# Reordered weight copies and splits around the first two experts of an attention, routing and expert kernel, with later float-form jobs and a shorter mask set-up

## The chip, the cores and the metric

The kernel runs on one core of a Trainium2 chip. The metric is the device time of one execution in microseconds (us). Engines are named as in the profile: PE (TensorE, matmuls), PEld (its weight loads), DVE (VectorE), ACT (ScalarE), POOL (GpSimd) and SP (SyncE, which here only issues DMAs). Each engine works through its own list of instructions in the order in which the program was written.

## What is computed

Cut to what matters, the reference is a gated linear attention, a routed layer of eight experts, and a dense layer:

```python
# attention: B=2, H=8, S=768, D=48
for t in range(S):
    state = alpha[:, :, t, :, None] * state + einsum('bhd,bhe->bhde', k[:, :, t], v[:, :, t])
    y[:, :, t] = einsum('bhd,bhde->bhe', q[:, :, t], state)
x = y as 1536 tokens of 384 numbers
# routing: E=8 experts, each with F=1024 hidden units
e(i) = argmax(x[i] @ w_gate);  g(i) = its softmax weight
out[i] = g(i) * (relu(x[i] @ w1[e]) @ w2[e])      # tokens over an expert's capacity give 0
# dense layer, 384 -> 2048 -> 384
h = out @ w_in
result = (h * tanh(softplus(h))) @ w_out
```

## The kernel before, in words

Everything is float32. A product of two float32 numbers is made on PE from three products of shorter ones: each operand is split into a high part and a low part, and high times high, low times high and high times low are added up. A weight **piece** of 128x768 numbers is loaded into a tile `st[i]`; ACT copies it to its high part `whi[i]` (`conv_high`, L337 to L345), DVE subtracts the two and leaves the low part `wlo[i]` (`conv_low`, L347 to L350). Each expert has eight pieces, the even ones for its first product (`w1`), the odd ones for its second (`w2`); each serves two steps.

The program has three parts.

- **Attention and routing.** Twelve tiles of 128 tokens go through the attention and get an expert and a place. ACT writes a check value for each tile into `chk`. The rows of x, scaled by the gate, are scattered to a table `tab` in DRAM, sorted by expert. The last tile's share of expert 0 doesn't go through DRAM: PE adds it with matmuls of a one-hot matrix (`slot_split`, L846), on a split of the last tile's rows that ACT (`xg_lh`, L838) and DVE (`xg_ll`, L839) make.
- **Experts.** For each expert e a window of 240 rows is gathered from `tab` (`gather`, issued on SP, L124), transposed on PE (L1072) and split into `xh` (ACT, L1089) and `xl` (DVE, L1090), all of it by `xpose(e)`. Then come eight **steps** (e, m). A step issues `g1(e, m)` (nine matmuls at L1100, into one PSUM bank of two that alternate), whose result ACT turns into `hh` (L1104) and DVE into `hl` (L1105), and `g2` of three steps earlier (nine matmuls at L1117, which need that step's `hh` and `hl`). Steps are counted 0 to 63.
- **Dense layer.** `f1` (L1181) and `f2` (L1224) on pieces 64 to 79. `f_mish` (L1193 to L1199 on ACT) and `gated(b)` (L1209 to L1211 on DVE) stand between them; the first steps of `f1` overlap the last expert's.

Work that isn't tied to a step is slipped in by hand. The program turns off the scheduler (`manual_schedule`), so the order in which the Python code calls things is the order on each engine:

- The weights of the dense layer come as 64-bit words and are brought to **float forms** by twelve jobs. `cvt_a(n)` is ACT's Square (L198) and Relu (L233) and two bit operations on DVE (L201, L204); `cvt_b(n)` is one more bit operation on DVE (L209) and a store to DRAM (L241, tensors `wi_s` and `wo_s`) issued on SP. The list `free` (L1353) gives the steps that may take a job, and the jobs are spread over them.
- `load_to` (L327) issues the loads `st[i]` on SP (L331). Pieces 64 to 71 are read from `wi_s` and `wo_s`, so `load_to` holds back pieces 68 to 71 until all twelve `cvt_b` are issued (`written`, L324).
- `check_tiles` (L782) reduces `chk` on DVE to one number per partition, `cm`; `check_all` (L789), called in step 7, transposes `cm` on PE (L791) and reduces it further, for a flag that is read near the end.
- `tot` (L1055) is a small matmul that counts tokens per expert; `mxc`, `places` and `sort_places` turn it into offsets on DVE.

Of the kernel before, what the change touches and what calls it, by code (L numbers as in the profile page):

```python
# [10 lines left out]
F32 = mybir.dt.float32  # L11
# [4 lines left out]
AF = mybir.ActivationFunctionType  # L16
ALU = mybir.AluOpType
AX = mybir.AxisListType
# [5 lines left out]
def kernel(  # L24
# [18 lines left out]
    nc = tc.nc  # L43
# [3 lines left out]
    E = w1.shape[0]  # L47
# [5 lines left out]
    NTILE = NT // C  # L53
    HP = H // 2
    HS = 64
    R2 = HS + D
    SW = 2 * D + E
    KD = DM // 128
    MF = FF // 128
# [6 lines left out]
    ATT = 4  # L66
# [8 lines left out]
    const = ctx.enter_context(tc.tile_pool(name="const", bufs=1))  # L75
# [8 lines left out]
    def w_new(i):  # L84
        p = wr_p[2 if i >= 76 else (i + 8) % 12 < 8]
        whi[i], wlo[i] = (p.tile([128, PW], F32R, tag=t, name=f"{t}{i}") for t in ("whi", "wlo"))
# [135 lines left out]
    def cvt_load(n):  # L222
        if n < len(cvt_jobs):
            t = words(fpool[0].tile([128, 2 * CN], F32, tag="big", name="w64", bufs=3)[:, 0:2 * cvt_jobs[n][1].shape[1]])
            nc.sync.dma_start(out=t, in_=words(cvt_jobs[n][0]))
            cvt_t[n] = [t]
# [94 lines left out]
    ahead = [WST + 4]  # L321
# [5 lines left out]
    def load_to(n):  # L327
        while load_n[0] < min(n, len(pieces)) and cvt_n[0] >= written(load_n[0]):
            i = load_n[0]
            st = raw_p[i % 14 >= 8].tile([128, PW], F32, tag="st", name=f"st{i}")  # L330
            nc.sync.dma_start(out=st.rearrange("p (a b) -> p a b", b=pieces[i].shape[2]), in_=pieces[i])  # L331
            wst_t[i] = st
            load_n[0] += 1

    low = []

    def conv_high(n):  # L337
        while conv_n[0] < min(n, len(pieces)):
            i = conv_n[0]
            load_to(i + 1 + ahead[0])  # L340
            w = wst_t.pop(i)
            w_new(i)
            nc.scalar.activation(out=whi[i], in_=w, func=AF.Copy)  # L343
            low.append((i, w))
            conv_n[0] += 1  # L345

    def conv_low(only=None):  # L347
        for i, w in [x for x in low if only in (None, x[0])]:
            nc.vector.tensor_tensor(out=wlo[i], in0=w, in1=whi[i].bitcast(F32), op=ALU.subtract)  # L349
            low.remove((i, w))  # L350
# [13 lines left out]

    with ExitStack() as actx:
        ap_ = actx.enter_context(tc.tile_pool(name="att", bufs=1))
        chk = ap_.tile([128, NTILE], F32, name="chk")
        nc.vector.memset(chk, 0.0)
        neg1 = ap_.tile([128, 1], F32, name="neg1")
        nc.vector.memset(neg1, -1.0)  # L370
# [2 lines left out]
        sel = ap_.tile([128, HP, SW], F32, name="sel")  # L373

        tri_f = ap_.tile([128, 128], F32, name="tri_f")
        seen_f = ap_.tile([128, 128], F32, name="seen_f")
        seen = ap_.tile([128, 128], I32, name="seen")
        io_i = ap_.tile([128, E], I32, name="io_i")
        slot_i = ap_.tile([128, WIN], I32, name="slot_i")
# [1 line left out]
        def route_consts():  # L381
            nc.gpsimd.memset(tri_f, 1.0)
            nc.gpsimd.affine_select(
                out=tri_f, in_=tri_f, pattern=[[1, 128]], compare_op=ALU.is_gt,
                fill=0.0, base=0, channel_multiplier=-1,
            )
            nc.gpsimd.memset(ones, 1.0)
            nc.gpsimd.memset(seen_f, -1.0)
            nc.gpsimd.affine_select(
                out=seen_f, in_=seen_f, pattern=[[1, 128]], compare_op=ALU.is_ge,  # L390
                fill=0.0, base=0, channel_multiplier=-1,
            )
            nc.gpsimd.iota(io_i, pattern=[[-1, E]], base=E - 1, channel_multiplier=0)
            nc.gpsimd.iota(slot_i, pattern=[[1, WIN]], base=(E - 1) * NT, channel_multiplier=0)
            nc.gpsimd.iota(tokid, pattern=[[C, NTILE]], base=0, channel_multiplier=1)

        def route_copies():
            nc.scalar.activation(out=tri, in_=tri_f, func=AF.Copy)
            nc.scalar.activation(out=seen, in_=seen_f, func=AF.Copy)
            nc.scalar.activation(out=down, in_=io_i, func=AF.Copy)  # L400
            nc.scalar.activation(out=firsts, in_=io_i[0:1], func=AF.Copy, scale=float(NT))
            nc.scalar.activation(out=slots, in_=slot_i, func=AF.Copy)
# [64 lines left out]
        def heads(t):  # L467
            return t.rearrange("p (j c) -> p j c", j=HP)
# [45 lines left out]

        def k_scale(i):
            kp = sp.tile([128, HP, C], F32, tag="kp", name="kp")
            nc.vector.scalar_tensor_tensor(
                out=kp[0:R2], in0=heads(kn_t.pop(i))[0:R2], scalar=-1.0 if i == NTILE - 1 else 1.0,
                in1=rt_t.pop(i)[0:R2], op0=ALU.mult, op1=ALU.mult,
            )  # L520
            kp_t[i] = kp

        def q_scale(i):
# [258 lines left out]
        def check_tiles():  # L782
            ok = const.tile([128, NTILE], F32, name="ok")
            nc.vector.tensor_scalar(out=ok, in0=chk, scalar1=NEWTON_TOL, scalar2=None, op0=ALU.is_le)
            cm = const.tile([128, 1], F32, name="cm")
            nc.vector.tensor_reduce(out=cm, in_=ok, axis=AX.X, op=ALU.min)
            return cm
# [63 lines left out]
        def slot_hot(i):  # L851
            last = i == NTILE - 1
            hot_t[i] = mid_tile("hot_last")[:, 0:WIN].bitcast(F32R) if last else ap_.tile([128, WIN], F32, name=f"hot{i}")
            nc.vector.tensor_scalar(out=hot_t[i], in0=slots, scalar1=sl_l[i], scalar2=None, op0=ALU.is_equal)
# [186 lines left out]
        low_x = split_x(i)  # L1041
        route_rank(i)
        slot_hot(i)
        low_x()
        route_x(i)
        route_slot(i)
        cm = check_tiles()
        count(i + 1)
        route_c(SLOT1)
        conv_high(ATT - 1)  # L1050
        conv_low(0)
        slot_split()
        del xs_t[0]
        tot = rk[:, E:2 * E]
        nc.tensor.matmul(out=tot, lhsT=ones, rhs=pre[pre_n[0] % 2], start=True, stop=True, skip_group_check=True)  # L1055


    wr_p.append(main.enter_context(tc.tile_pool(name="wr1", bufs=8)))
# [77 lines left out]
    def y_out(e):  # L1136
        y_put(4 + e % 2 * 2, off_v.pop(e), free=e == E - 1)
# [8 lines left out]
    def places():  # L1146
        nc.vector.tensor_tensor_scan(out=inc, data0=tot, data1=zn[:, 0:E], initial=0.0, op0=ALU.add, op1=ALU.add)
        nc.vector.tensor_tensor(out=off, in0=inc, in1=tot, op=ALU.subtract)
        nc.vector.tensor_copy(out=meta_i, in_=off)
        nc.vector.scalar_tensor_tensor(out=inc, in0=down, scalar=-float(NT), in1=off, op0=ALU.mult, op1=ALU.add)  # L1150
# [191 lines left out]
    CVT_END = 45  # L1342
    LATE_AHEAD = 3
    xpose(0, False)
    nc.vector.tensor_reduce(out=mxc, in_=tot, axis=AX.X, op=ALU.max)
    conv_low(2)
    conv_high(ATT)
    scatter(tab, si_last, xg_last, E * NT, "tab")
    gather(1)
    pend = []  # L1350
    job_at = {}

    free = [s for s in range(3, E * MF) if s % MF != 5 and (s % MF != 2 or s < MF)]  # L1353
    for n in range(2 * len(cvt_jobs)):
        job_at.setdefault(free[n * CVT_END // (2 * len(cvt_jobs))], []).append(((cvt_a, cvt_b)[n % 2], n // 2))
    for e in range(E):
        for m in range(MF):
            step = e * MF + m
            if m == 6:
                off_v[e] = place(e)  # L1360
            g1(e, m)
            pend.append((e, m))
            if len(pend) > LAG:
                pe, pm = pend.pop(0)
                g2(pe, pm)
                if pm == MF - 1:
                    y_out(pe)
            if e == E - 1 and m >= MF - EARLY:
                n = m - MF + EARLY
                (f_head if m < MF - 1 else f1_at)(n)  # L1370
            conv_high(min(step + 1 + LEAD, ATT + step * 9 // 8, E * NP1 + 3))
            if step:
                conv_low({1: 1, 2: 4}.get(step))
            for f, n in job_at.get(step, ()):
                f(n)
                if f is cvt_b:
                    cvt_load(n + 3)
            if step == 4:
                places()
            if step == 5:  # L1380
                sort_places()
            if step == 7:
                check_all(cm)
                slow_at()
            if step % 4 == 3 and 0 < step // 4 <= NTILE:
                tok_scatter(step // 4 - 1)
            if e == E - 1 and m == 0:
                nc.sync.dma_start(
                    out=srt, in_=toks.rearrange("(c p) o -> p (c o)", p=128), allow_slow_non_contiguous=True
                )  # L1390
            if E * MF - EARLY - 1 - LATE_AHEAD <= step < E * MF - EARLY - 1:
                late_load(step - (E * MF - EARLY - 1 - LATE_AHEAD))
            if step == E * MF - 4:
                cvt_marks()
            if step == E * MF - 2:
                cvt_flag()
            if m == (5 if e else 6) and e + 1 < E:
                xpose(e + 1)
                if e + 2 < E:
                    gather(e + 2)  # L1400
    for pe, pm in pend:
# [242 lines left out]
```

## Time and profile before

| | us |
|---|---|
| median of 3 runs (lowest to highest) | 421.44 (421.35 to 422.85) |
| the profiled execution's own time | 421.35 |
| its span in the profile | 419.6 |
| PE busy | 406.4 (97%) |
| PE weight loads busy | 374.5 (89%) |
| DVE busy | 323.9 (77%) |
| ACT busy | 324.5 (77%) |
| POOL busy | 58.6 (14%) |
| chain that ended last | PE 89%, DVE 5%, ACT 2% |

The span is the time between the first and the last instruction that the profiler saw; 1.75 us of the execution lie around it. A busy share is an average over the three parts of the program. The attention part lasts to about 70 us, the experts from about 75 to 217 us, and the dense layer and the output from there to the end.

### The profile page before, as it was taken

What the parts mean: (1) busy time and instruction counts of PE and PEld (TensorE: products, weight loads), DVE (VectorE), ACT (ScalarE), POOL (GpSimd) and SP (SyncE); (2) the same over time, 40 slices, a digit from 0 to 9 for tenths busy, and PEclk for the clock granted to TensorE, in tenths of its full rate; (3) what the DMA queues carried; (4) which work ended last, traced back from release to release, by engine and by line L of the source; (5) the groups of instructions that cost most, each with busy time, mean ns of one, the idle gap of its engine ahead of it and who ended that gap; (6) DMA issues with size and microseconds to landing.
All of it is one profiled execution on the core that took longest, in us unless ns stands there. A gap on an engine that the chain in (4) does not pass through costs nothing.

```text
span 419.6 us, 8354 instructions
## 1 busy us (share of the span) xinstructions
PE 406.4 (97%) x3111; PEld 374.5 (89%) x3114; DVE 323.9 (77%) x645; ACT 324.5 (77%) x572; POOL 58.6 (14%) x77
## 2 busy tenths in 40 slices
PE   7899999899999999999999999999999999999993
PEld 3798998899999999999999899989898988889893
DVE  7999997899989888988649877867786775565361
ACT  5889997877868677777499987888788869797630
POOL 5222573101101012100000000000000000012043
PEclk9999999999999999999999999999999999999998
DMA  7999996999999999944525000211110000001022
GB/s 236 351 290 334 347 382 224 352 354 235 341 322 285 303 313 283 287 128 125 187 80 174 15 1 0 52 63 39 37 41 1 0 2 0 2 19 57 2 77 80
DMA packets 50541, 67.31 MB, mean 160 GB/s; under 512 B 5372, under 2 KB 41212, under 8 KB 50492
## 3 DMA queue, kind: packets, MB, share of 16 engines
q1 hardware_dynamic: 48572, 61.97, 47.9%
q0 software_dynamic: 1920, 4.73, 3.1%
q8 instruction: 26, 0.43, 0.4%
q14 instruction: 23, 0.19, 0.1%
HBM read 55.86 MB, written 10.83 MB: 159 GB/s over the span
## 4 chain that ended last, share of the span: by engine, by line
PE 89%; DVE 5%; ACT 2%; issue 1%; DMA 1%; POOL 0%; POOLq 0%; DVEq 0%; ACTq 0%
PE bk L1224 24%; PE bk L1181 24%; PE bk L1117 14%; PE bk L1100 14%; PE bk L537 3%; PE bk L589 2%; PE bk L605 2%; PE bk L578 2%; DVE wlo L349 1%; PE bk L557 1%; PE bk L613 1%; PE bk L1072 1%; DMA an<-in_alpha_t_dram 1%; DVE hl L1105 0%; PE bk L868 0%
## 5 line engine op out<-in xcount | busy, mean ns | idle before, releaser
L349 DVE TENSOR_TENSOR wlo<-st,whi 128x768 fp32r<-128x768 f32 x72 | 68.2, 953 | 12.4 <-ACT whi L343 9.9
L1209 DVE TENSOR_TENSOR p<-p,bk 128x512 f32<-128x512 f32 x48 | 32.8, 683 | 43.6 <-ACT p L1199 43.6
L1224 PE MATMUL bk<-whi,big 128*128 128x384 f32 x240 | 66.4, 337 | 0.0
L343 ACT ACTIVATE whi<-st 128x768 fp32r<-128x768 f32 x72 | 60.1, 841 | 0.0
L1193 ACT ACTIVATE p<-bk 128x512 f32<-128x512 f32 x48 | 28.8, 599 | 32.0 <-PE bk L1181 28.6
L1117 PE MATMUL bk<-hl,whi 128*128 128x240 f32 x192 | 52.9, 276 | 0.0
L1117 PE MATMUL bk<-hh,wlo 128*128 128x240 f32 x192 | 52.7, 275 | 0.0
L1117 PE MATMUL bk<-hh,whi 128*128 128x240 f32 x192 | 52.7, 274 | 0.0
L1224 PEld LDWEIGHTS bk<-whi,big 128*128 128x128 f32 x240 | 44.1, 188 | 1.5
L1104 ACT ACTIVATE hh<-bk 128x240 fp32r<-128x240 f32 x64 | 23.5, 367 | 28.2 <-PE bk L1100 25.3
L108 POOL DMA_INDIRECT out_dram<-acc,srt x12 | 12.2, 1018 | 225.5 <-DVE acc L1248 221.1
L1181 PE MATMUL bk<-x2l,whi 128*128 128x512 f32 x144 | 41.6, 397 | 0.0
L1181 PE MATMUL bk<-x2h,wlo 128*128 128x512 f32 x144 | 41.2, 394 | 0.0
L1181 PE MATMUL bk<-x2h,whi 128*128 128x512 f32 x144 | 41.1, 394 | 0.0
L1224 PE MATMUL bk<-wlo,big 128*128 128x384 f32 x120 | 40.6, 338 | 0.0
L1117 PEld LDWEIGHTS bk<-hl,whi 128*128 128x128 f32 x192 | 36.4, 189 | 0.2 <-DVE hl L1105 0.2
L1117 PEld LDWEIGHTS bk<-hh,whi 128*128 128x128 f32 x192 | 36.3, 189 | 0.0
L1117 PEld LDWEIGHTS bk<-hh,wlo 128*128 128x128 f32 x192 | 36.3, 189 | 0.0
L1100 PE MATMUL bk<-xh,whi 128*128 128x240 f32 x192 | 33.0, 280 | 1.7 <-ACT xh L1089 1.6
L1181 PEld LDWEIGHTS bk<-x2h,wlo 128*128 128x128 f32 x144 | 27.0, 188 | 6.7
L1181 PEld LDWEIGHTS bk<-x2l,whi 128*128 128x128 f32 x144 | 27.0, 188 | 6.4
L1100 PE MATMUL bk<-xl,whi 128*128 128x240 f32 x192 | 32.1, 276 | 0.4 <-DVE xl L1090 0.4
(238 smaller groups left out, 955.4 us busy)
## 6 DMA issues: line engine op xcount, KB each, us to landing
st<-in_w_dram SPq DMA_DIRECT2D x64, 384.0 KB, 7.9
qn<-in_q_t_dram SPq DMA_DIRECT2D x12, 256.0 KB, 5.4
kn<-in_k_t_dram SPq DMA_DIRECT2D x12, 256.0 KB, 7.1
w<-in_w_in_dram SPq DMA_DIRECT2D x6, 512.0 KB, 7.4
w<-in_w_out_dram SPq DMA_DIRECT2D x6, 512.0 KB, 6.4
sd<-in_w_in_dram SPq DMA_DIRECT2D x8, 384.0 KB, 4.1
sd<-in_w_out_dram SPq DMA_DIRECT2D x8, 384.0 KB, 4.7
tab<-zero SPq DMA_DIRECT2D x4, 720.0 KB, 6.5
```

Source lines behind the costliest of these rows:

```text
L108: r = nc.gpsimd.indirect_dma_start(out=dst[:, :], out_offset=bass.IndirectOffsetOnAxis(ap=idx, axis=0), in_=src, in_offset=None, bounds_ch ...
L343: nc.scalar.activation(out=whi[i], in_=w, func=AF.Copy)
L349: nc.vector.tensor_tensor(out=wlo[i], in0=w, in1=whi[i].bitcast(F32), op=ALU.subtract)
L537: nc.tensor.matmul(out=sc_t[i][r][:, j], lhsT=kp[p, j, :], rhs=qq[p, j, :], start=True, stop=True)
L578: nc.tensor.matmul(out=ot_at(j, r), lhsT=s2f[half(r), j * D:j * D + w], rhs=q2[i % 2][half(r), j, :], start=(j % 2 == 0), stop=False, skip ...
L1100: nc.tensor.matmul(out=hps, lhsT=a[:, kk], rhs=b_[:, kk, :], start=(n == 0), stop=(n == 3 * KD - 1))
L1104: nc.scalar.activation(out=hh, in_=hps, func=AF.Relu)
L1117: nc.tensor.matmul(out=y[n], lhsT=a[:, ns], rhs=b_, start=(m == 0 and t == 0 and n % 2 == 0), stop=(m == MF - 1 and t == 2), skip_group_ch ...
L1181: r = nc.tensor.matmul(out=hps, lhsT=a[:, kk], rhs=b_[:, kk, w0:w0 + wd], start=(n == 0), stop=(n == 3 * KD - 1))
L1193: nc.scalar.activation(out=p, in_=h2_t[b], func=AF.Sigmoid, scale=-1.0)
L1209: nc.vector.tensor_tensor(out=g, in0=g, in1=h2_t.pop(b), op=ALU.mult)
L1224: nc.tensor.matmul(out=o_t[c], lhsT=a[:, ts], rhs=b_, start=(m in (0, MA) and n == 0), stop=(m in (MA - 1, MF2 - 1) and n == 2),)
```

## The change

The changed kernel computes the same, with these edits:

- The body of `conv_high` becomes a function `high(i)`, so that pieces can be taken out of order. In the front (the stretch between the last tile of the attention and the first expert) ACT copies piece 2 between `xg_lh` and `xg_l`, piece 1 after `xpose(0)`, and piece 3 in step 0. On DVE `wlo[0]` is made before the count.
- The `tot` matmul goes from the front to behind `g1(0, 0)`, the reduction `mxc` to step 4.
- The jobs for float forms start at step 5 of the list `free`, not 3, and are spread over the same number of places: the first `cvt_a` is in step 6, the last `cvt_b` goes from step 60 to step 63.
- `xpose(1)` stands right behind `g2` in step 6, ahead of that step's weight copy; `place(0)` goes from step 6 to step 7.
- `check_tiles` is called in step 7, just ahead of `check_all`, not in the front.
- `k_scale` (L515) uses a plain multiply for all tiles but the last; the mask `seen` is built as int32 on POOL, without a float mask and ACT's copy.

```diff
+    def high(i):
+        load_to(i + 1 + ahead[0])
+        w = wst_t.pop(i)
+        w_new(i)
+        nc.scalar.activation(out=whi[i], in_=w, func=AF.Copy)
+        low.append((i, w))
+        conv_n[0] += 1
+
     def conv_high(n):
         while conv_n[0] < min(n, len(pieces)):
...
+            high(conv_n[0])
...
-        chk = ap_.tile([128, NTILE], F32, name="chk")
+        chk = const.tile([128, NTILE], F32, name="chk")
...
-            nc.gpsimd.memset(seen_f, -1.0)
+            nc.gpsimd.memset(seen, -1)
             nc.gpsimd.affine_select(
-                out=seen_f, in_=seen_f, pattern=[[1, 128]], compare_op=ALU.is_ge,
-                fill=0.0, base=0, channel_multiplier=-1,
+                out=seen, in_=seen, pattern=[[1, 128]], compare_op=ALU.is_ge,
+                fill=0, base=0, channel_multiplier=-1,
             )
...
-            nc.scalar.activation(out=seen, in_=seen_f, func=AF.Copy)
...
-            nc.vector.scalar_tensor_tensor(
-                out=kp[0:R2], in0=heads(kn_t.pop(i))[0:R2], scalar=-1.0 if i == NTILE - 1 else 1.0,
-                in1=rt_t.pop(i)[0:R2], op0=ALU.mult, op1=ALU.mult,
-            )
+            kn, rt = heads(kn_t.pop(i))[0:R2], rt_t.pop(i)[0:R2]
+            if i < NTILE - 1:
+                nc.vector.tensor_tensor(out=kp[0:R2], in0=kn, in1=rt, op=ALU.mult)
+            else:
+                nc.vector.scalar_tensor_tensor(out=kp[0:R2], in0=kn, scalar=-1.0, in1=rt, op0=ALU.mult, op1=ALU.mult)
...
         slot_hot(i)
+        high(2)
         low_x()
         route_x(i)
         route_slot(i)
-        cm = check_tiles()
+        conv_low(0)
         count(i + 1)
         route_c(SLOT1)
-        conv_high(ATT - 1)
-        conv_low(0)
         slot_split()
         del xs_t[0]
         tot = rk[:, E:2 * E]
-        nc.tensor.matmul(out=tot, lhsT=ones, rhs=pre[pre_n[0] % 2], start=True, stop=True, skip_group_check=True)
...
     xpose(0, False)
-    nc.vector.tensor_reduce(out=mxc, in_=tot, axis=AX.X, op=ALU.max)
     conv_low(2)
-    conv_high(ATT)
+    high(1)
     scatter(tab, si_last, xg_last, E * NT, "tab")
     gather(1)
...
-    free = [s for s in range(3, E * MF) if s % MF != 5 and (s % MF != 2 or s < MF)]
+    free = [s for s in range(5, E * MF) if s % MF != 5 and (s % MF != 2 or s < MF)]
...
-            if m == 6:
+            if m == (6 if e else 7):
                 off_v[e] = place(e)
...
+            if step == 6:
+                xpose(1)
...
+            if step == 0:
+                nc.tensor.matmul(out=tot, lhsT=ones, rhs=pre[pre_n[0] % 2], start=True, stop=True, skip_group_check=True)
             if step == 4:
+                nc.vector.tensor_reduce(out=mxc, in_=tot, axis=AX.X, op=ALU.max)
                 places()
...
             if step == 7:
-                check_all(cm)
+                check_all(check_tiles())
                 slow_at()
...
             if m == (5 if e else 6) and e + 1 < E:
-                xpose(e + 1)
+                if e:
+                    xpose(e + 1)
                 if e + 2 < E:
                     gather(e + 2)
```

What the edits do to the order on the engines shows at three places. Line numbers of the changed program are a few lower or higher than before; the operations are the same.

**The front, ACT.** The rows run from `xg_lh` to the first `hh` of the experts. Before:

```order
L838 ACTIVATE xg_lh_180<-bk3_89,gt_1307 128x384
L764 ACTIVATE xg_l1_169<-bk3_89,gt_1307 128x384
L343 ACTIVATE whi1_1326<-st1_791 128x768
L343 ACTIVATE whi2_1329<-st2_793 128x768
L1089 ACTIVATE xh_1361<-bk0_86 128x2x240
L1089 ACTIVATE xh_1361<-bk1_87 128x240
L343 ACTIVATE whi3_1375<-st3_883 128x768
L1104 ACTIVATE hh_1393<-bk2_88 128x240
```

With the change:

```order
L839 ACTIVATE xg_lh_179<-bk3_89,gt_1305 128x384
L341 ACTIVATE whi2_1313<-st2_791 128x768
L765 ACTIVATE xg_l1_168<-bk3_89,gt_1305 128x384
L1088 ACTIVATE xh_1351<-bk0_86 128x2x240
L1088 ACTIVATE xh_1351<-bk1_87 128x240
L341 ACTIVATE whi1_1360<-st1_789 128x768
L1103 ACTIVATE hh_1378<-bk2_88 128x240
L341 ACTIVATE whi3_1386<-st3_881 128x768
```

One weight copy stands between `xg_lh` and `xg_l`, and none between `xg_l` and `xh`.

**Step 7, PE and DVE.** On PE the transpose of `cm` stands between `g2(0, 4)` and `g1(1, 0)` in both programs. Before (the last rows of `g2`, the transpose, the first row of `g1`):

```order
L1117 MATMUL bk_91<-hh,wlo_1432 128x240
L1117 MATMUL bk_91<-hl,whi_1431 128x240
L791 MATMUL bk_93<-ident,cm 1x128
L1100 MATMUL bk_88<-xh,whi_1531 128x240 [waits DVE_49,Activation_49]
L1100 MATMUL bk_88<-xh,whi_1531 128x240
```

With the change:

```order
L1116 MATMUL bk_91<-hh,wlo_1425 128x240
L1116 MATMUL bk_91<-hl,whi_1424 128x240
L792 MATMUL bk_93<-ident,cm 1x128 [waits DVE_49]
L1099 MATMUL bk_88<-xh,whi_1515 128x240 [waits Activation_49]
L1099 MATMUL bk_88<-xh,whi_1515 128x240
```

On DVE `ok` and `cm` stood in the front, ahead of `wlo[0]`. With the change they stand in step 7 (`hl_1594` is `hl` of step (0, 7), `wt_1564` the first job's word):

```order
L351 TENSOR_TENSOR wlo9_1561<-st9_1083,whi9_1560 128x768
L201 TENSOR_SCALAR wt_1564<-w64_1345 128x512
L204 SCALAR_TENSOR_TENSOR wt_1564<-w64_1345,wt_1564 128x512
L1142 TENSOR_LOAD meta_i_106
L1104 SCALAR_TENSOR_TENSOR hl_1594<-bk3_89,hh_1593 128x240
L351 TENSOR_TENSOR wlo10_1609<-st10_1085,whi10_1608 128x768
L209 SCALAR_TENSOR_TENSOR wt_1564<-w64_1345,wt_1564 128x512
L785 TENSOR_SCALAR ok_1616<-chk_127 128x12
L787 TENSOR_REDUCE cm_1618<-ok_1616 128x1
```

The transpose on PE now waits for DVE, and `cm` stands behind the low parts, `hl` of step (0, 7) and the bit operations of the first job.

**The last steps, DVE and SP.** The last job's L209 (`wt_3423`) with the change, on DVE around `hl` of step (7, 7), which is `hl_3537`:

```order
L351 TENSOR_TENSOR wlo67_3522<-st67_3048,whi67_3521 128x768
L254 SCALAR_TENSOR_TENSOR slow_i_109<-bk5_91,slow_f_110 1x1
L1104 SCALAR_TENSOR_TENSOR hl_3537<-bk3_89,hh_3536 128x240
L209 SCALAR_TENSOR_TENSOR wt_3423<-w64_3021,wt_3423 128x512
L1208 TENSOR_TENSOR p_3463<-p_3463,bk0_86 128x512
```

And the end of SP's list of loads with the change:

```order
L272 DMA sd3_3519<-in_w_out_dram 128x768
L241 DMA wo_s_119<-wt_3423 128x512
L331 DMA st68_3615<-wi_s_118 128x3x256
L331 DMA st69_3617<-wo_s_119 128x2x384
L331 DMA st70_3619<-wi_s_118 128x3x256
```

Before, L209 of the last job (`wt_3337`) stood three steps earlier on DVE, behind `wlo66`. On SP the last store stands right ahead of the loads of pieces 68 to 71 in the changed program; before, one other load (`sd3`) lay between them.

## Rows read from the trace of the kernel before

**Rows 1.** Windows: PE, PEld, DVE, ACT, POOL busy (instructions), PEclk, DMA share, GB/s.

```profile
75.43:91.97 16.54, 16.07 (x135) 15.50 (x136) 15.28 (x33) 12.02 (x24) 0.98 (x1) 1.00 1.04 364
91.97:405.00 313.03, 313.03 (x2030) 293.22 (x2029) 239.69 (x429) 249.74 (x401) 21.08 (x19) 1.00 0.40 118
412.60:416.00 3.40, 0.00 (x0) 0.00 (x0) 0.56 (x1) 0.00 (x0) 0.98 (x1) 1.00 0.36 124
416.00:419.60 3.60, 0.00 (x0) 0.00 (x0) 0.00 (x0) 0.00 (x0) 0.00 (x0) 0.50 0.02 5
```

**Rows 2.** Timeline of PE in the front: start, duration, what, [idle before].

```profile
73.27 0.50 PE L846 MATMUL bk<-hot_last,xg_ll 128*128 128x240 f32 x3
...
75.43 0.64 PE L1100 MATMUL bk<-xh,whi 128*128 128x240 f32 x3 [1.65 <-ACT xh L1089]
```

**Rows 3.** Timeline of ACT in the front.

```profile
73.36 1.56 ACT L343 ACTIVATE whi<-st 128x768 fp32r<-128x768 f32 x2
74.82 0.82 ACT L1089 ACTIVATE xh<-bk 128x480 fp32r<-128x480 f32 x2
```

**Rows 4.** Timeline of PE in steps 6 to 8.

```profile
87.21 0.78 PE L1072 MATMUL bk<-ident,xs 128*128 128x128 f32 x6
87.75 0.58 PE L1100 MATMUL bk<-xh,whi 128*128 128x240 f32 x3
...
89.85 0.27 PE L791 MATMUL bk<-ident,cm 128*1 128x128 f32 x1
...
91.81 0.28 PE L1117 MATMUL bk<-hh,whi 128*128 128x240 f32 x1
...
92.82 0.50 PE L1100 MATMUL bk<-xh,whi 128*128 128x240 f32 x3
```

**Rows 5.** Timeline of DVE: the check in the front, a low part and L209 in step 4.

```profile
72.82 0.17 DVE L784 TENSOR_SCALAR ok<-chk 128x12 f32<-128x12 f32 x1
73.02 0.17 DVE L786 TENSOR_REDUCE cm<-ok 128x1 f32<-128x12 f32 x1
...
84.94 0.95 DVE L349 TENSOR_TENSOR wlo<-st,whi 128x768 fp32r<-128x768 f32 x1
85.81 0.69 DVE L209 SCALAR_TENSOR_TENSOR wt<-w,wt 128x512 uint32<-128x512 uint32 x1
```

**Rows 6.** Timeline of ACT: the first job's two passes.

```profile
81.04 0.67 ACT L198 ACTIVATE wm<-w 128x512 f32<-128x512 f32 x1
81.74 0.72 ACT L233 ACTIVATE wm<-wm,small 128x512 f32<-128x512 f32 x1
```

**Rows 7.** Timeline of SP: the last store and the load of piece 68.

```profile
203.32 0.34 SPq L241 DMA_DIRECT2D wo_s<-wt  x1
...
204.19 0.45 SPq L331 DMA_DIRECT2D st<-wi_s  x1
```

**Rows 8.** The tile `st` in the stretch 204.1 to 205, which holds that load alone.

```profile
DMA to landing us min/median/max: 4.1/4.1/4.1
```

**Rows 9.** Timeline of ACT: the copy of piece 68.

```profile
218.49 0.86 ACT L343 ACTIVATE whi<-st 128x768 fp32r<-128x768 f32 x1
```

**Rows 10.** Timeline of DVE: `hl` of step (7, 7), and the end of the third `gated`.

```profile
215.85 0.38 DVE L1105 SCALAR_TENSOR_TENSOR hl<-bk,hh 128x240 fp32r<-128x240 f32 x1
...
226.58 0.69 DVE L1211 TENSOR_TENSOR big<-p,big 128x512 fp32r<-128x512 f32 x1
```

**Rows 11.** Timeline of PE: the start of the third `f2`.

```profile
227.68 0.34 PE L1224 MATMUL bk<-whi,big 128*128 128x384 f32 x1
```

**Rows 12.** Lines by form, PE, 1.2 to 6.3: line engine op, names, shapes xcount | busy us, mean ns | idle before.

```profile
L799 PE MATMUL bk<-busy 128*128 128x512 bf16 x12 | 5.3, 630 | 1.3 <-DVE busy L138 1.3
```

**Rows 13.** Lines by form, PE, 216 to 219.3.

```profile
L1181 PE MATMUL bk<-x2h,whi 128*128 128x512 f32 x3 | 0.9, 395 | 0.0
```

**Rows 14.** Lines by form, DVE, 8 to 64: the two ways of multiplying in attention.

```profile
L517 DVE SCALAR_TENSOR_TENSOR kp<-kn,rt 112x512 f32<-112x512 f32 x11 | 8.5, 769 | 0.0
L524 DVE TENSOR_TENSOR q<-qn,pt 112x512 f32<-112x512 f32 x11 | 7.5, 683 | 0.0
```

More of the change, by code (lines that the diff above doesn't have):

```diff
@@ L335 @@
     low = []
+    def high(i):
[5 more added lines that the diff above has]
+        conv_n[0] += 1
     def conv_high(n):
         while conv_n[0] < min(n, len(pieces)):
[L339 to L345, printed above, removed]
+            high(conv_n[0])
     def conv_low(only=None):
@@ L375 @@
         tri_f = ap_.tile([128, 128], F32, name="tri_f")
-        seen_f = ap_.tile([128, 128], F32, name="seen_f")
         seen = ap_.tile([128, 128], I32, name="seen")
```

## The prediction

> **What bounds the kernel now.** I read the windows first: they tell in which stretch PE is short of work. From 91.97 to 405 us PE is busy for all of 313.03 us; from 75.43 to 91.97 for 16.07 of 16.54 [rows 1]. So between the experts' first steps and the output only what makes PE wait can change the time, and what other engines do is free until it does. Then PE's timeline, to find where it waits: in the front it sits idle for 1.65 us before the first `g1`, released by ACT's `xh` [rows 2]. The timelines of ACT and DVE tell what those engines did meanwhile, and that of SP when the loads go out. The sum is made against the profiled execution, 421.35 us, which is 0.09 below the median of 421.44.
>
> How much PE loses in the first steps has to be counted, since most of it is small. From 91.81 to 92.82 one `g2` passes without a stall, 1.01 us [rows 4]; `g1` has nine matmuls of the same width and costs the same. Between the first `g1` at 75.43 and `g2(0, 5)` at 91.81 lie nine `g1` and five `g2`, 14.14 us, the transposes of the second window, 0.54 (87.21 to 87.75), and the one of `cm`, about 0.1: 14.78. It took 16.38, so 1.60 us are stalls.
>
> **The front, a gain.** PE's last matmul of `slot_split` ends at 73.27 + 0.50 = 73.77 [rows 2]. ACT then still has half of two weight copies to do (1.56 us from 73.36), and `xh` starts at 74.82 [rows 3]. With the change no copy stands there, so `xh` starts at about 73.80: the first `g1` moves from 75.43 to 74.4, a gain of 1.0. If ACT reached the place late for another reason it could be 0.5; more than 1.05 it can't be, because `slot_split` doesn't move.
>
> **The small stalls, a gain.** The jobs for float forms no longer stand among the first weight copies, and the second window is gathered sooner. At most all 1.60 us go; I take 1.25 of them before step 7, and nothing as the lower end.
>
> **The check, a loss.** This is the part that decides. Before, `cm` was made at 73.02 [rows 5], and PE's transpose of it at 89.85 waited for nothing [rows 4]. Now the transpose waits for DVE, and all later matmuls are queued behind it. I follow the chain that leads to `cm`. Without stalls the transposes of the second window end at 74.4 + 11 x 1.01 + 0.1 + 0.54 = 86.15 (seven `g1`, four `g2`, `tot`); with the 0.35 of stalls that I keep, at 86.5. From there, in the order that the front part shows and by durations:
>
> - ACT: `xh` of the window 0.82 [rows 3], `whi9` 0.78 (half of 1.56), Square 0.7 and Relu 0.8 with its read-out (0.67 and 0.72 [rows 6]), `hh(0, 7)` 0.4 (taken as `hl`'s 0.38 [rows 10]), `whi10` 0.78: 4.28 us
> - DVE behind it: `wlo10` 0.95, L209 0.69, `ok` 0.2, `cm` 0.17 [rows 5]: 2.0 us
>
> That is 6.3 us, less 0.3 since neighbours on an engine overlap at their ends: `cm` at 92.5. PE meanwhile has `g1(0, 7)` and `g2(0, 4)`, 2.02 us, and is done at 88.5. It idles for **4.0 us**; the transpose and `g1(1, 0)` follow, and `g2(0, 5)` starts at 92.5 + 0.1 + 1.1 = 93.7, where it started at 91.81 before. The front, the stalls and the check together are so a **loss of 1.9 us**. A lower end: the transposes end at 86.15 and the chain takes 5.6, `g2(0, 5)` at 92.9, a loss of 1.1. An upper one: the second window is transposed no earlier than before, by 87.75, and the chain takes the full 6.3; 95.2, a loss of 3.4. What the front gains only makes PE reach the wait sooner. While PE stands, ACT and DVE catch up, so I expect no more stalls in the next steps.
>
> **The last job, a loss.** The loads of pieces 68 to 71 are issued only behind the store of the twelfth job. Before, the store was issued at 203.32 and the load of piece 68 at 204.19 [rows 7]; it landed 4.1 us later [rows 8], at 208.3, and ACT copied it at 218.49 [rows 9], with ten microseconds to spare. Now the job's last bit operation stands on DVE behind `hl(7, 7)`, which runs from 215.85 for 0.38 [rows 10]; with 0.69 for itself [rows 5] it ends at 216.9. The store is issued then and the load 0.4 later, at 217.3. It can land at 221.4 if it takes 4.1 again. It then shared the DMAs with two other transfers, now only with the store, so I take 3.3, landing at 220.6; the ends are 219.7 and 221.4. ACT, which takes things in order, waits at the copy for 220.6 - 218.5 = 2.1 us, and everything behind it on ACT and DVE moves by that, up to the third `gated`. Its last row ends at 226.58 + 0.69 = 227.27 [rows 10], and the third `f2` starts at 227.68 [rows 11]: 0.4 us to spare, and I allow 0.2 more, an estimate, for waits of ACT for PE on the way. **Loss: 1.5 us**, from 0.6 to 2.3. The piece behind it, 69, waits for the store to land besides; ACT wants it 5.2 us after piece 68, so it is hidden. The bit operation also pushes the first `gated` back by 0.69, which its own slack takes.
>
> **What I cost at nothing.** A plain multiply in place of the scaled one: 683 against 769 ns a time [rows 14], eleven times on DVE; the longer mean would give 0.95 us on DVE, but PE, which the chain names, doesn't wait for it in most tiles. The mask on POOL and ACT's copy less are hidden by the wait for the first inputs; without that cover ACT would win a few tenths of a microsecond. `tot` behind `g1(0, 0)` costs what it cost before. The jobs moved by three steps load ACT by 1.5 us in steps 60 and 61, where PE has three steps of `hh` ahead; without that lead it would be 1.5 more.
>
> **Sum.** 421.35 + 1.9 + 1.5 = **424.75**, say 424.8 us, 0.8% slower. A measurement of this kernel tells about 0.5%, 2.1 us, from no change.
>
> **The rivals.**
>
> - *Faster.* PE isn't held at the check and piece 68 lands in time. Then the 1.0 of the front and up to 1.6 of stalls remain: 418.7 us. It needs `cm` by 88.5, before PE has done `g2(0, 4)`. For it speaks that all edits of the front aim at the rows in which PE idles; against it the order on DVE, in which `cm` stands behind `hl(0, 7)`, whose input PE itself makes only at 87.5. With only the last job's loss added it would be 420.3. Together a chance of 0.1.
> - *One loss only.* PE is held at the check, but piece 68 lands by 219 and costs nothing: 423.2. Or the check costs 0.3 and piece 68 costs 1.5: 423.1. The landing time of a lone load isn't in the rows, which speaks for the first. Chance 0.2, about half way into "no change".
> - *The clock falls in the 4.0 us at the check.* At the end of this trace PE stopped at about 412.6; its granted clock was still 1.00 up to 416.0, then 0.50 [rows 1], that is 1.2 instead of 2.4 GHz. The 1.65 us of the front [rows 2] didn't lower it. At the start twelve matmuls of 512 columns took 630 ns each, 5.3 us in all [rows 12], where such a matmul takes 395 at full clock [rows 13]. If PE's work ran at half speed for as long, 5.3 us of it would do the work of 2.65: up to 2.65 us more, and if for three quarters of that, 2.0. The time would be 426.8. For it speaks the fall at the end of the trace, against it that no idle inside the kernel has lowered the clock so far. Chance 0.2.
> - *The change doesn't do what it says:* the second window doesn't arrive sooner, and the check comes late by 3.4: 426.3. It is inside the forecast's range.
>
> The Trainium skill bears on the third rival. Its page "TensorE: Matmul & The Clock Gate", in Part 1, "The HAM clock gate", says that the throttled state is the default, that activity releases it and that idleness brings it back. By that rule the wait at the check would cost its own 4 us and a slow stretch behind it, and the sum would be 426.8 in place of 424.8. The trace agrees that idleness ends at 0.50 [rows 1]; whether it does so here no row of before shows.
>
> **How the numbers follow.** The forecast, both losses at full clock, has a chance of 0.5 and runs from 423.1 (1.1 and 0.6) to about 426. The clock adds 425.5 to 427.5. One loss only reaches down to about 422, the faster rival from 420.3 to 418.7. I leave out the fastest tenth and a little at the top: 421.2 to 427.4. Faster by over 0.5% (under 419.3): 0.08. Within 0.5% (up to 423.5): the rest of the first rival, most of the second and the lowest part of the forecast, 0.25. Slower: 0.67.
>
> **What would show it.** In the new profile: the first `g1` at about 74.4, with `xh` right behind `slot_split`; an idle of about 4 us on PE before the transpose of `cm`, released by DVE's `cm`; full clock behind it; the load of piece 68 issued at about 217 plus the shift, with ACT idle for 2 us before its copy, and PE idle for 1 to 2 us in the first steps of the dense layer. I am wrong if `cm` comes early, if PE's busy share stays at 16 of 16.5 us in the first steps, or if PE passes the copy of piece 68 without an idle.

## The result and the profile after

The changed kernel is slower: 428.62 us in the median of six runs (426.19 to 428.89), against 422.14 for the kernel before on the same chip (421.35 to 426.46). The ratio is 1.0134, with an interval from 1.0100 to 1.0168. The direction was forecast; the size was not, and the time lies 1.2 us above the forecast's range. The profiled execution took 428.88 us, its span is 427.1, and as before 1.8 us lie around it.

First the windows of the changed kernel, PE alone (busy, instructions, granted clock, DMA share, GB/s), to be read against [rows 1]. The stretch begins with the first `g1` and ends in step 9.

```profile
74.31:87.55 13.24, 12.08 (x101) 1.00 0.90 303
86.00:90.40 4.40, 4.35 (x40) 1.00 1.05 359
90.40:92.00 1.60, 0.00 (x0) 1.00 1.08 373
92.00:93.00 1.00, 0.00 (x0) 0.81 1.08 390
93.00:94.30 1.30, 0.00 (x0) 0.50 1.08 315
94.30:96.40 2.10, 2.08 (x11) 0.50 1.15 266
96.40:98.32 1.92, 1.92 (x11) 0.50 0.91 229
98.32:99.88 1.56, 1.56 (x11) 0.64 0.80 226
99.88:108.95 9.07, 9.07 (x83) 1.00 0.77 156
```

Two things are to be seen. PE does nothing from 90.4 to 94.3, and while it does nothing its granted clock falls from 1.00 to 0.50. The matmuls that follow run at 0.50 until about 99. And in the first row PE is busy for only 12.08 of 13.24 us, where it should have had fewer stalls than before.

The timeline of PE at the check answers to [rows 4]:

```profile
87.55 0.78 PE L1071 MATMUL bk<-ident,xs 128*128 128x128 f32 x6
88.09 0.58 PE L1099 MATMUL bk<-xh,whi 128*128 128x240 f32 x3
...
94.32 0.37 PE L792 MATMUL bk<-ident,cm 128*1 128x128 f32 x1 [3.97 <-DVE cm L787]
94.34 0.97 PE L1099 MATMUL bk<-xh,whi 128*128 128x240 f32 x3
95.12 0.84 PE L1099 MATMUL bk<-xh,wlo 128*128 128x240 f32 x3
95.76 0.84 PE L1099 MATMUL bk<-xl,whi 128*128 128x240 f32 x3
96.40 0.41 PE L1116 MATMUL bk<-hh,whi 128*128 128x240 f32 x1
```

The transpose that waited for nothing at 89.85 now waits 3.97 us for `cm`; the forecast had 4.0. Behind it three matmuls take 0.84 us where the same three took 0.50, and `g2(0, 5)` starts at 96.40, where it started at 91.81. The timeline of DVE shows `cm` at the end of the chain that the forecast followed:

```profile
92.42 0.96 DVE L351 TENSOR_TENSOR wlo<-st,whi 128x768 fp32r<-128x768 f32 x1 [0.16 <-ACT whi L341]
93.29 0.69 DVE L209 SCALAR_TENSOR_TENSOR wt<-w,wt 128x512 uint32<-128x512 uint32 x1
93.90 0.17 DVE L785 TENSOR_SCALAR ok<-chk 128x12 f32<-128x12 f32 x1
94.10 0.17 DVE L787 TENSOR_REDUCE cm<-ok 128x1 f32<-128x12 f32 x1
```

The list of ACT's waits (engine and line, what it waited for: us in total, times, longest) names two that the kernel before didn't have:

```profile
ACT whi L341 <- DMA st<-wi_s: 2.1, 1, 2.1
ACT whi L341 <- DMA tab<-xg_l,si_all: 2.0, 1, 2.0
```

The first is the copy of piece 68, forecast at 2.1 us. SP's and ACT's rows around it answer to [rows 7, 9]:

```profile
222.84 0.33 SPq L241 DMA_DIRECT2D wo_s<-wt  x1
223.22 0.43 SPq L331 DMA_DIRECT2D st<-wi_s  x1
```

```profile
226.67 0.85 ACT L341 ACTIVATE whi<-st 128x768 fp32r<-128x768 f32 x1 [2.06 <-DMA st<-wi_s]
```

The load is issued 0.4 us behind the store and ACT starts 3.45 us after that; forecast 3.3, an estimate that no row of before gave, so its closeness is in part luck. The second wait was in nobody's account: in step 1 the copy of piece 4 waits for the first of the two last scatters to `tab`.

```profile
79.27 0.85 ACT L341 ACTIVATE whi<-st 128x768 fp32r<-128x768 f32 x1 [2.04 <-DMA tab<-xg_l,si_all]
```

Since PE works without a pause in most of the program, where the time went can be read from four marks on its timeline: the first `g1`, the transposes of the second window, those of the third window, and the last matmul.

| stretch, us | before | changed | difference |
|---|---|---|---|
| start to first `g1` | 75.43 | 74.31 | -1.12 |
| first `g1` to transposes of window 2 | 11.77 | 13.24 | +1.47 |
| window 2 to window 3 | 15.71 | 21.40 | +5.69 |
| window 3 to last matmul | 309.65 | 310.97 | +1.32 |
| behind the last matmul, and around the span | 8.78 | 8.95 | +0.17 |

The sum is 7.53 us, which is the difference of the two profiled executions. These stretches serve for the experiments too, since the attention ahead of them takes 1 to 3 us more on some of the chips (there the first `g1` comes at 76.7 to 78.0). Each ratio below is to the kernel before on the same chip.

### The profile page after: what moved, and what is told of

Its sections match the earlier page's. It is cut to its first block, busy times and chain, and to the rows that moved or that the text cites. A ratio compares the mean times of both kernels' runs of the same rounds, so it can differ in the third digit from the quotient of the medians.

```text
span 427.1 us, 8358 instructions
## 1 busy us (share of the span) xinstructions
PE 410.4 (96%) x3114; PEld 376.6 (88%) x3114; DVE 325.3 (76%) x645; ACT 324.8 (76%) x571; POOL 59.1 (14%) x77
## 4 chain that ended last, share of the span: by engine, by line
PE 87%; ACT 4%; DVE 4%; DMA 3%; issue 1%; POOL 0%; POOLq 0%; SPq 0%; ACTq 0%; DVEq 0%
PE bk L1223 23%; PE bk L1180 22%; PE bk L1099 14%; PE bk L1116 14%; PE bk L538 3%; PE bk L606 3%; PE bk L590 3%; PE bk L579 2%; DMA tab<-xg_l,si_all 2%; PE bk L558 1%; PE bk L1071 1%; PE bk L614 1%; DVE wlo L351 1%; DMA st<-wi_s 1%; ACT whi L341 1%
## 5 line engine op out<-in xcount | busy, mean ns | idle before, releaser
L1099 PE MATMUL bk<-xh,whi 128*128 128x240 f32 x192 | 33.9, 286 | 1.6 <-issue 0.9
L1104 DVE SCALAR_TENSOR_TENSOR hl<-bk,hh 128x240 fp32r<-128x240 f32 x64 | 25.8, 403 | 10.1 <-ACT hh L1103 10.0
L1099 PE MATMUL bk<-xh,wlo 128*128 128x240 f32 x192 | 32.5, 278 | 0.2 <-DVE wlo L351 0.2
```

Of the source, the lines that this page charges most:

```text
L1099: nc.tensor.matmul(out=hps, lhsT=a[:, kk], rhs=b_[:, kk, :], start=(n == 0), stop=(n == 3 * KD - 1))
L1104: nc.vector.scalar_tensor_tensor(out=hl, in0=hps, scalar=0.0, in1=hh.bitcast(F32), op0=ALU.max, op1=ALU.subtract)
```

## The experiments

**The check back in the front** (`e1_check_front`), the changed kernel with

```diff
         route_slot(i)
+        cm = check_tiles()
         conv_low(0)
...
-                check_all(check_tiles())
+                check_all(cm)
```

> The changed kernel with check_tiles back in the front, so that cm is ready long before its transpose; all else as changed. Theory (the wait for cm and the slow clock behind it): PE no longer idles 4.0 us and the clock stays full, which gives back 3.6 + 2.4 = 6.0 us: 422.6 us against 428.6. Rival (ACT and DVE are late in these steps anyway, so that PE meets another wait behind the check): half of it or less comes back, 425.5 to 427.

Measured: 0.9986 (0.9970 to 1.0001), window 2 to window 3 in 15.86 us. The whole of the 5 us is gone from that stretch and no other wait took its place. (The first `g1` to window 2 takes 11.59 us here, so the wait at piece 4 is missing from this profile too, and the fall from 1.0134 to 0.9986 isn't the check's alone.) The transpose on PE's timeline waits for nothing and the next `g1` is at its heels:

```profile
91.36 0.27 PE L1117 MATMUL bk<-hl,whi 128*128 128x240 f32 x1
91.47 0.27 PE L792 MATMUL bk<-ident,cm 128*1 128x128 f32 x1
91.50 0.59 PE L1100 MATMUL bk<-xh,whi 128*128 128x240 f32 x3
```

**The last job in step 60 again** (`e2_last_job`) and **both repairs** (`e3_both`):

```diff
-    CVT_END = 45
+    CVT_END = 43
```

> The changed kernel with the jobs for float forms spread over 43 places instead of 45, so that the last one ends in step 60 as before, not 63; the check stays late. Theory (piece 68 lands late): ACT's 2.06 us wait at its copy goes and with it 1.5 us: 427.1 us. Rival (the third f2 would wait for something else there): 428.6 us, no change.

> Both repairs at once: the check's cm from the front and the last job in step 60. Theory: the two add up, 428.6 - 6.0 - 1.5 = 421.1 us, about the kernel before, since the front's reorder has not moved the later steps. Rival (the reorder of the front is worth its 1.0 to 2.6 us once nothing holds PE): 418.8 to 420.4 us.

Measured: 1.0066 (1.0043 to 1.0088) and 0.9944 (0.9924 to 0.9964). Window 3 to the last matmul takes 309.54 us in both, 310.84 in the first experiment: the late job costs **1.3 us**. ACT's wait for `st<-wi_s` is gone from its list. With both repairs the kernel is faster than before, as the rival of the recorded expectation had it and not its theory: the front's gain is there once nothing takes it back; repeated on two other chips it was 0.9961 and 0.9956.

**PE kept at work while it waits** (`e4_busy`):

```diff
+                keep_busy(bk[6], 16)
                 check_all(check_tiles())
```

> The changed kernel with 16 matmuls of 512 columns without use put on PE ahead of the check's transpose, so that PE works while it waits for cm (they take about 16 x 0.23 = 3.7 us, less than the wait). Theory (the clock falls because PE idles): the granted clock stays 1.00 behind the check and 2.4 us come back, 426.2 us, while the wait itself stays. Rival (the slow stretch has another cause, or the clock falls all the same): 428.6 us and 0.5 behind the check.

Measured: 1.0055 (1.0040 to 1.0071). The windows of PE around the check show full clock, and its timeline shows the matmuls put in (one record is missing) and the rest of the wait:

```profile
91.00:95.00 4.00, 3.93 (x22) 1.00 1.05 360
95.00:98.00 3.00, 2.49 (x22) 1.00 1.09 358
```

```profile
91.74 3.40 PE L800 MATMUL bk<-busy 128*128 128x512 bf16 x15
95.65 0.27 PE L792 MATMUL bk<-ident,cm 128*1 128x128 f32 x1 [0.51 <-DVE cm L787]
95.67 0.58 PE L1099 MATMUL bk<-xh,whi 128*128 128x240 f32 x3
96.09 0.50 PE L1099 MATMUL bk<-xh,wlo 128*128 128x240 f32 x3
```

Window 2 to window 3 takes 18.99 us. So the wait alone costs 18.99 - 15.86 = **3.1 us**, and the slow clock the rest: **2.4 us** in the first profile (21.40), 1.6 in the second experiment's (20.60), and from 1.35 to 2.55 over all eight profiles with the changed front and the idle left empty (20.34 to 21.54). The clock falls because PE idles, and useless matmuls prevent it; they don't shorten the wait: the transpose starts 6.8 us behind those of window 2 with them (88.87 to 95.65) as without (87.55 to 94.32). Nine profiles, with the one of `e5_check_late`, have the empty idle and a stretch at 0.50 behind its start; the eleven others have no such stretch there.

The clock need not fall while PE stands. In five of the nine it fell 0.7 to 1.3 us after PE was back at work, as in `a_third`, where the transpose starts at 95.04; in these five the low stretch was short and cost 1.6 us.

```profile
92.00:94.00 2.00, 0.00 (x0) 1.00 1.08 371
94.00:96.00 2.00, 0.96 (x9) 1.00 1.09 309
96.00:98.00 2.00, 2.00 (x11) 0.50 1.07 345
98.00:100.00 2.00, 2.00 (x13) 0.65 1.02 311
```

**The changed kernel beside both repairs, the attention's edits undone, and the front's order undone** (`a_changed`, `e3_again`, `e7_attn_old`, `e8_front_old`, on one chip). The third is both repairs with the scaled multiply, the float mask and ACT's copy of it put back. The fourth is both repairs with

```diff
-        high(2)
...
+        conv_high(ATT - 1)
+        conv_low(0)
         slot_split()
...
-    high(1)
+    conv_high(ATT)
```

> The changed kernel itself, beside the next three on one chip. Theory: tr to tr (from the transposes of the second window to those of the third) takes 20.6 to 21.4 us as in its first trace, of which 5 to 5.5 are the check and the slow clock; 1.3 to 1.7% slower than before. Rival (the second step group's wait of 2.04 us for the scatter, seen in its first trace, is part of it): the stretch from the first g1 to those transposes takes 13.2 us again, not 11.6.

> Both repairs (cm from the front, last job in step 60), again, as the base of the next two. Theory: the same 0.5 to 0.6% faster than the kernel before as the first time. Rival (the first time was this chip's spread): no difference, 0.998 to 1.002.

> Both repairs, with the edits in the attention undone (the scaled multiply for all tiles, the float mask and ACT's copy). Theory: these edits are hidden, so the time is that of both repairs within 0.3 us. Rival (DVE is what attention waits for): 0.5 to 1 us slower than both repairs, the plain multiply's 86 ns in eleven tiles.

> Both repairs, with the order of the front undone (pieces 1 and 2 copied between xg_l and xh, wlo of piece 0 behind them). Theory: the first g1 comes 1.0 us later after slot_split (1.65 us idle instead of 0.6) and the time is 1.0 to 1.3 us above that of both repairs. Rival (another wait, such as that for the scatter, takes the gain back in the next steps): within 0.3 us of both repairs.

Measured: 1.0130 (1.0113 to 1.0147), 0.9961 (0.9947 to 0.9976), 0.9975 (0.9965 to 0.9985) and 0.9985 (0.9961 to 1.0009); medians 429.89, 423.22, 423.54 and 424.27 us. The attention's edits make 0.3 us between the medians, inside the spread: hidden, as costed, as far as this can tell. The front's order is worth 1.05 us between the medians. (The two profiled executions, 423.64 and 423.38 us, don't show it, since the attention ahead took longer in the first.) PE's rows say why. Both repairs, then the front's order undone:

```profile
77.83 0.64 PE L1100 MATMUL bk<-xh,whi 128*128 128x240 f32 x3 [0.67 <-ACT xh L1089]
```

```profile
77.61 0.64 PE L1100 MATMUL bk<-xh,whi 128*128 128x240 f32 x3 [1.63 <-ACT xh L1089]
```

Here the changed kernel took 11.59 us from the first `g1` to window 2, not 13.24: the wait at piece 4 doesn't come in every execution. It met its loss of 1.3% on this chip without it.

**The transpose two steps later** (`e9_step9`), with the last job in step 60:

```diff
-                check_all(check_tiles())
-                slow_at()
+                cm = check_tiles()
+            if step == 9:
+                check_all(cm)
+                slow_at()
```

> The changed kernel with the last job in step 60, cm still made on DVE in step 7, but its transpose on PE two steps later, in step 9. Theory (only the place of the transpose in PE's list is at fault, not the two small DVE instructions): PE passes step 7 without an idle and the time is that of both repairs, 0.3 to 0.6% under the kernel before. Rival (ok and cm on DVE in step 7 hold the weight splits back): 1 to 3 us slower than that.

Measured: 0.9983 (0.9952 to 1.0015), median 420.46 against 421.34. PE passes the transpose without an idle and at full clock:

```profile
92.81 0.27 PE L792 MATMUL bk<-ident,cm 128*1 128x128 f32 x1
```

On DVE `cm` is done at 92.65, so the two steps are only just enough. Window 2 to window 3 takes 16.13 us, 0.3 more than with the check in the front. So it is almost wholly the place in PE's list that counted: the same `cm` from the same place on DVE costs 0.3 us when PE asks for it two steps later, and 4.5 to 5.7 when it asks at once.

**The two edits alone, in the kernel before** (`e5_check_late`, `e6_job_late`; the first also moves `chk` to memory that outlives the attention, the second spreads the jobs over 47 places, so that the last falls in step 63), **and the changed kernel again** (`a_again`):

> The kernel before with one edit: cm made in step 7, just ahead of its transpose. Theory: PE waits at the transpose from 89.85 until cm is made behind hl(0, 7), the low part of piece 10 and the second job's two operations, at about 94.1; g2(0, 5) starts 3.4 us later, and the clock falls behind the idle for another 1.6 to 2.4: 5.0 to 5.8 us slower than before (1.012 to 1.014). Rival (the wait hurts only beside the moved front and jobs): under 2 us.

> The kernel before with one edit: the jobs for float forms spread over 47 places of the list, so that the last one ends in step 63, not 60. Theory: piece 68 lands late, the third f2 waits, and 1.3 us are lost (1.003). Rival (no change): 0.999 to 1.001.

> The changed kernel once more. Theory: without a wait for the scatter, first g1 to the second window's transposes takes 11.6 us and the loss is 1.3% or a little under; with it (ACT idle for about 2 us before the copy of piece 4), that stretch takes 13.2 us and the loss is 1.6 us more. Rival (that wait belongs to the change and comes in each execution): 13.2 us.

Measured: 1.0132 (1.0097 to 1.0168), 1.0069 (1.0043 to 1.0094) and 1.0116 (1.0079 to 1.0153). Moving the check alone makes the kernel before about as slow as the whole change. Its transpose and the windows behind it:

```profile
94.14 0.37 PE L791 MATMUL bk<-ident,cm 128*1 128x128 f32 x1 [4.12 <-DVE cm L786]
```

```profile
92.00:94.00 2.00, 0.00 (x0) 0.54 1.09 387
94.00:96.00 2.00, 1.86 (x10) 0.50 1.17 290
96.00:98.00 2.00, 2.00 (x11) 0.50 0.59 114
98.00:100.00 2.00, 2.00 (x15) 0.75 0.68 29
```

The late job alone lost more than forecast, and its list of ACT's waits says how:

```profile
ACT whi L343 <- DMA st<-wi_s: 2.1, 1, 2.1
ACT whi L343 <- DMA tab<-xg_l,si_all: 2.0, 1, 2.0
```

The first `g1` to window 2 takes 13.70 us there, 11.77 in the check's run on the same chip, and the front's order is that of before in both. So the wait at piece 4 doesn't need the change's front; it came in the late job's profile, and in the changed kernel's second one on this chip (13.53).

**What holds the scatter up** (`a_third`, `e10_loads_late`, `e3_third`, `e11_both_loads_late`, then `a_fourth`, `e10_again`). In the traces of the chips where the wait shows, the scatter races with three loads of 512 KB for the first jobs:

| trace | scatter starts | first load issued | landed behind start | piece 4 waits |
|---|---|---|---|---|
| check late | 72.22 | 73.54 | 3.3 | no |
| transpose in step 9 | 72.54 | 73.41 | 4.7 | no |
| before | 72.75 | 73.52 | 3.8 | no |
| changed, second time | 72.76 | 73.28 | 6.9 | 2.3 us |
| changed | 72.76 | 73.27 | 6.4 | 2.0 us |
| job late | 73.12 | 73.53 | 7.1 | 2.0 us |

So the loads were put behind the gather of the second window, hence behind the scatter, in the changed kernel and in both repairs:

```diff
-    for n in range(3):
-        cvt_load(n)
...
     gather(1)
+    for n in range(3):
+        cvt_load(n)
```

> The changed kernel, as the base of the next run. Theory: where the scatter starts 0.5 us or less ahead of the three 512 KB loads, it lands over 6 us after its start and the stretch from the first g1 to the second window's transposes takes 13.2 us; where it starts 0.8 us or more ahead, under 5 us and 11.6. Rival (the wait has another cause): no such relation.

> The changed kernel with the three 512 KB loads for the first jobs issued behind the gather of the second window, so behind the scatter; all else as changed. Theory (these loads hold the scatter up): the scatter lands within 4 us of its start, ACT never waits for it at piece 4, the stretch takes 11.6 us, and the time is 1.6 us lower wherever the changed kernel shows 13.2. Rival (the scatter is slow by itself): 13.2 us and the time of the changed kernel.

> Both repairs (cm from the front, last job in step 60), as the base of the next run. Theory: 0.3 to 0.6% under the kernel before, 1.6 us more where the scatter's wait shows.

> Both repairs, and the three loads behind the gather as well. Theory: 11.6 us in each execution, so 1.0 to 1.4 us under the kernel before (0.997) with less spread than without. Rival (the later loads make the first jobs late on ACT and DVE): no faster than both repairs.

> The changed kernel again, base of the next run on a further chip. Theory: where the scatter starts 0.5 us or less ahead of the three 512 KB loads, the stretch from the first g1 to the second window's transposes takes 13.2 us, elsewhere 11.6.

> The changed kernel with the three loads behind the gather, again. Theory: 11.6 us in that stretch whatever the base shows, and 1.6 us less than the base if that shows 13.2. Rival: as slow as the base in that stretch.

Measured, in this order: 1.0106 (1.0077 to 1.0136), 1.0096 (1.0061 to 1.0130), 0.9956 (0.9943 to 0.9969), 0.9956 (0.9937 to 0.9975), and on a further chip 1.0104 (1.0068 to 1.0140) and 1.0114 (1.0082 to 1.0147). All six profiles show 11.6 us in the stretch: on both chips the wait didn't come in the base either, so the pairs tell nothing of its cause. What they do tell: issuing the loads later neither helps nor costs there. The relation of the table was half met again: in the eleven other profiles with the loads in their old place the scatter starts 1.5 to 2.8 us ahead of the first load, and none shows the wait; a short gap, with the wait expected, did not come again. That the loads hold the scatter up is a guess from these traces and **stays open**.

## Why the prediction was right and wrong

| term, us | forecast | measured |
|---|---|---|
| front, idle of PE before the first `g1` | -1.0 | -0.97 in the first profile; -1.05 by the medians without it |
| front, stalls and check together, full clock | +1.9 | +2.1 (11.60 + 18.99 - 27.48, less 1.0) |
| late job | +1.5 | +1.3 |
| slow clock behind the check | 0, with a rival of 2.0 | +1.35 to +2.55 |
| wait for the scatter at piece 4 | not named | +1.65 and +1.9 in two of the changed kernel's five profiles, 0 in three |
| the attention's edits | 0 | 0.3 between medians, inside the spread |

Right were the two losses and their mechanisms. The idle at the check was forecast at 4.0 us and is 3.97; the chain behind window 2, forecast at 6.0 us, took 6.2 (88.09 to 94.32). The wait of ACT for piece 68 was forecast at 2.1 and is 2.06, and PE paid 1.3 of it. The rival on the other side, a faster kernel at 418.7, fell with the order on DVE, as argued against it. That the check alone decides the sign is shown by `e1_check_front` and `e5_check_late`: taken out of the changed kernel it leaves no loss, put into the kernel before it makes one of 1.3%.

Wrong was the step that gave the falling clock "Chance 0.2" and took both losses "at full clock" for the likeliest. In all nine profiles with the idle of about 4 us at the check left empty, the clock fell to 0.50 (1.2 GHz) and matmuls behind the check ran at that level. In four of them it fell while PE stood, as the rival's words have it, in five only when PE was back at work. The price of that rival was near, 2.0 against 1.35 to 2.55; its chance should have been the larger one, and the forecast 426.8. What the Trainium skill's page "TensorE: Matmul & The Clock Gate" says in Part 1, "The HAM clock gate", that idleness brings the throttled state back, the traces bear out in each of those profiles, and the run with useless matmuls bears it out from the other side: clock 1.00 at the check, 1.35 to 2.55 us less. The one row that spoke against it [rows 2] was a shorter idle, of 1.65 us, and was weighed as if it were alike.

The rest of the miss, in the first profile, is the wait for the scatter: 428.88 is 424.75 from the forecast's sum, with 2.4 for the clock and 1.65 for the scatter, 428.80. Neither alone would have left the forecast's range (427.15 and 426.4). On the three chips where the changed kernel's profile shows no such wait its median lay 4.4 to 5.3 us above that of before, here 6.5. The list of before had named no such wait because ACT came to piece 4 at 78.18, when the scatter, which started at 72.75 and took 3.8 us, had been down since 76.55. The forecast brought ACT to that place 1 us sooner and never asked what else the copy waits for there. But the trace of before would not have answered: with 1.6 us to spare ACT could come 1 us sooner and still not wait. What made the wait is that the scatter itself took 6.4 us, and `e6_job_late` shows that with the old front, where ACT came at 78.2 as before and waited 2.0 us. The one warning in the trace of before is that its second scatter took 6.8 us to land. Why the scatter sometimes takes 6.4 to 7.1 us and sometimes 3.3 to 4.7 isn't settled.

One part of the sum was also misread without harm: "I take 1.25 of them before step 7". From the first `g1` to window 2 before took 11.77 us for 11.11 of work, so at most 0.66 of the stalls lay there; with the change 0.4 of them are left. The other stalls lay behind the transposes, and both repairs still have them (15.84 us against 15.71). The end of the transposes came out where forecast all the same, 85.91 + 0.54 = 86.45 for a forecast of 86.5, in `e9_step9`, which has the changed front and did not meet the scatter's wait.

## What to carry to other kernels

A small instruction on the engine that sets the time is priced by what stands behind it: a transpose of one column cost about 5 us when its input was made late on a busy engine, and 0.3 us when it was asked for two steps later. An idle of PE is to be costed together with the clock behind it, here 1.35 to 2.55 us on top of 3.1. Slack that one trace shows behind a transfer is only as safe as the transfer's time is steady, and that takes more than one trace to see. And a job that others wait for through DRAM must not be the last of its list: look at which loads are held back until it is done.

## What the runs showed of the hardware

- The clock's fall is repeatable here. Nine profiles with a PE idle of 4.0 to 4.1 us inside the kernel show the granted clock at 0.50 in or just behind it; the idles of about 1.65 us in the front lowered it in none of the three profiles that have them. In the changed kernel it fell at about 93 while PE was still idle, and was back at 1.00 by 99.9, after 5 us of matmuls at the lower level; in five other profiles it fell only when PE was back at work.
- A long idle isn't the only thing that comes before a fall. In four profiles (`e2_last_job`, `e4_busy`, `e10_loads_late`, `a_fourth`) the clock stood at 0.50 once more, in the attention between 62 and 66.6 us, where no idle of PE just before was longer than 0.5 us. What lowered it there isn't shown; the stretches compared above begin behind it.
- Sixteen matmuls without use, put into the idle, saved 1.35 to 2.55 us of clock for a wait that stayed as long as it was.
- The same scatter of 128 rows landed at very different times behind its start in six profiles of kernels that issue nearly the same work around it, from 3.3 in `e5_check_late` to 7.1 in `e6_job_late`; in the profile of before the first took 3.8 and the next 6.8.
